# Two early blocks convolved in one burst of 64x32 tiles, with x copied inside SBUF, the channel taps made behind block 0, and half of one unit's stores on GpSimd's queue

## The chip, the cores and the metric

The kernel runs on one core of a Trainium2 chip. The core has a matrix engine (TensorE, PE in the profile; PEld is its weight load, which overlaps the matmuls), a vector engine (VectorE, DVE), a scalar engine (ScalarE, ACT), a general engine (GpSimd, POOL) and a queue engine (SyncE, SP), which issues DMAs here and computes nothing. GpSimd issues DMAs too. All DMAs run on the same 16 DMA engines. The metric is the device time of the whole program in microseconds; a lower time is better.

## The reference

```python
def _attn_ref(x, weight):                      # x (8, 4096, 192), weight (8, 7)
    w = softmax(weight, axis=-1)               # with 1e-9 added to the sum
    x_pad = np.concatenate([zeros((B, 6, D)), x], axis=1)
    idx = np.arange(S)[:, None] + np.arange(K)[None, :]
    x_unf = x_pad[:, idx, :].reshape(B, S, K, H, group)
    return np.einsum('hk,bskhg->bshg', w, x_unf).reshape(B, S, D)

def _moe_ref(x, w_gate, w_val, w_out):         # (32768, 192), (192, 1536) twice, (1536, 192)
    g = x @ w_gate
    return (g * (1.0 / (1.0 + np.exp(-g))) * (x @ w_val)) @ w_out
```

First a causal convolution over 7 tokens: 8 heads of 24 channels, one softmaxed tap vector for each head. Its result goes through a SwiGLU feed-forward layer with 192 channels and 1536 hidden units. The output has 32768 rows of 192 in fp32.

## The kernel before

The 32768 tokens are cut into 64 blocks of 512 tokens, and four blocks make a unit. The hidden units are cut into 12 chunks of 128. A step n is one chunk of one block: block n // 12, chunk n % 12. There are 768 steps.

In each step gate_val (lines 837 to 858) does six matmuls of 64 rows by 512 columns, three into a "gate" bank of PSUM and three into a "val" bank, two at a time in the two row halves of the array. ScalarE takes the Silu of the gate bank (L855), VectorE multiplies it with the val bank (L857). There are three gate and three val banks. The down projection of a block is done in four slots (slot, down, lines 862 to 938), one in every third step, with 24 short matmuls each (L872). So TensorE's steady work is three steps and a slot, over and over.

The input of gate_val is the convolved block with channels on the partitions, in three tiles xc0 to xc2. How it is made depends on the block:

- Blocks 0 and 1 (early, eturn): x is loaded in windows of 64 rows (52 tokens and 6 of overlap) into xe. TensorE convolves it with the matrices "wide" (64 rows, 64 columns; the taps are held as a high and a low fp16 part, index a, so two matmuls add up), ScalarE and VectorE copy the result from PSUM into tme, TensorE transposes it (L490), and the engines copy it into xc.
- Blocks 2 and 3 (early_pair, lines 415 to 456): the same from xp, in two bursts of 32 matmuls with 64x64 tiles (tile_position (64r, 64c), so four at a time). The first burst stands after step 13's gate_val, the second inside the slot of step 15. Each burst writes one gate and one val bank, and these are copied (L445, and L456 for a repeat of the first 64 channels). Block 2 is then turned by TensorE (eturn(2) at step 18). Block 3 goes to DRAM (eout, L463, at step 16) and comes back by DMA transposes (efetch, L473, at step 19).
- Blocks 4 to 7, unit 1 (conv_half, lines 515 to 556): x in windows of 32 rows (26 tokens and 6 of overlap), held twice, in partitions 0 to 31 and again in 32 to 63 (and 64 to 95, 96 to 127 for the second half). The matrix "band" holds the high parts of the taps in the first 32 rows and the low parts in the next 32, so that one matmul of 64 rows does both. Its tiles are 64x32, eight at a time. make_band (L363) copies band from wide on GpSimd. The halves run in the slots of steps 25 and 31; then nine stores write the result to DRAM (conv_out, L567 and L575, at steps 31 and 32), and twelve DMA transposes fetch it (fetch, L589, from step 32).
- Blocks 8 to 63 (units 2 to 15, "pooled"): x is cast to fp16 in DRAM by a GpSimd DMA (cast_x, L649), brought to channel-major tiles by DMA transposes (turn_x, L665), channels 128 to 191 of two blocks are joined in one tile (join_x, L669), and the seven taps are multiplied and added by ScalarE (L742), VectorE (L717) and GpSimd (L692, L707) with a tap for each channel. These channel taps are both_taps. They come from make_picks (L609, at step 34; it uses which and above, made by GpSimd at L210 and L218) and make_channel_taps (L620 and L627, at step 37): a matmul with a 0/1 matrix that gives each channel its head's taps.

Order. Every engine runs its instructions in the order of the program text: seq (line 73) chains each one to the one before it on its engine. DMAs stand in that order on the queue of the engine that issues them: SP has the stores, the transposes and the outputs, GpSimd has the loads that cast. A queue that waits holds all that follows on it. For the pooled units, planned (lines 782 to 809) says at which step a unit's DMAs and jobs are put in: for unit 2 cast 21, jobs 38, and ten times for its turns and joins (24 to 42). pooled_work takes ScalarE's and VectorE's part of the jobs one at a time in the chunks j of 1, 4, 7 and 10.

Loads at the start, on GpSimd's queue in this order: xe(0), weights 0 and 1, xe(1), weights 2, the output weights, then the four helper operations for which and above, xp (two loads), x16 of unit 1 (four loads, since both copies of each half come from DRAM), the four copies of make_band, and xs of unit 2.

Of the kernel before, what the change touches and what calls it, by code (L numbers as in the profile page):

```python
# [10 lines left out]
def kernel(  # L11
# [9 lines left out]
    nc = tc.nc  # L21
    fp32 = mybir.dt.float32
# [121 lines left out]
    def dup_x(u, queue=None):  # L144
        for r in range(2):
            p0 = Q * r
            seq(
                (queue or nc.sync).dma_start(
                    out=x16[u][p0 + 32 : p0 + 64], in_=x16[u][p0 : p0 + 32]
                )  # L150
            )
# [46 lines left out]
    load_w(0)  # L198
    load_w(1)
# [5 lines left out]
    which = {}  # L205
    above = {}
    for name, first, rows in (("c01", 0, P), ("c2", P, Q)):
        which[name] = small(f"which_{name}", [H, P], i32)
        seq(
            nc.gpsimd.iota(  # L210
                which[name],
                pattern=[[0, P // rows], [1, rows]],
                base=first,
                channel_multiplier=-grp,
            )
        )
        above[name] = small(f"above_{name}", [H, P])
        seq(nc.gpsimd.tensor_single_scalar(above[name], which[name], 0, op=ALU.is_ge))  # L218
    xp = cpool.tile([P, 2 * EG, D], fp16, tag="xp", name="xp", bufs=1)
    for r in range(2):  # L220
        windows(xp, Q * r, (2 + r) * TB, EO, 0, 2 * EG)
    x16_tile(1)
    for r in range(2):
        for low in (0, 32):
            load_x(1, r, low=low)
# [189 lines left out]
    def early_pair(hh):  # L415
        w = EG * grp
        if hh == 0:
            for e in (2, 3):
                tme[e] = cpool.tile([P, EG, 4 * Q], fp16, tag="tme", name="tme")
        banks = [  # L420
            ppool.tile([P, TB], fp32, tag=tag, name="cv") for tag in ("gate", "val")
        ]
        for t in range(4):
            h = 4 * hh + t
            for a in range(2):
                for c in range(2):
                    for r in range(2):
                        seq(
                            nc.tensor.matmul(  # L429
                                banks[r][Q * c : Q * c + Q, t * w : t * w + w],  # L430
                                wide[Q * r : Q * r + Q, a, h, :],
                                xp[
                                    Q * r : Q * r + Q,
                                    c : 2 * EG : 2,
                                    h * grp : h * grp + grp,
                                ],
                                start=(a == 0 and t == 0),
                                stop=(a == 1),
                                skip_group_check=True,
                                tile_position=(Q * r, Q * c),  # L440
                            )
                        )
        for r, copy in ((0, act), (1, dve)):
            seq(
                copy(  # L445
                    tme[2 + r][
                        :, :, 4 * grp * hh : 4 * grp * hh + 4 * grp
                    ].rearrange("p g (t e) -> p g t e", t=4),
                    banks[r][:, 0 : 4 * w].rearrange(
                        "p (t g e) -> p g t e", t=4, g=EG  # L450
                    ),
                )
            )
        if hh == 0:
            for e in (2, 3):
                seq(dve(tme[e][:, :, SL * Q : 4 * Q], tme[e][:, :, 0:Q]))  # L456

    def eout(e):
        scre[e] = dpool.tile([XW, 4 * Q], fp16, tag="scre", name="scre")
        rows = scre[e].rearrange("(g c j) d -> c j g d", c=2, j=EO)  # L460
        for c in range(2):
            seq(
                nc.sync.dma_start(  # L463
                    out=rows[c], in_=tme[e][Q * c : Q * c + EO, :, :]
                )
            )
# [12 lines left out]
    def eturn(b, where):  # L479
        tiles = [  # L480
            cpool.tile([P, XW], fp16, tag=f"xc{k}", name=f"xc{k}", bufs=8)
            for k in range(SL)
        ]
        turned = range(SL) if len(where) == SL else (0, 2)
        banks = {}
        for k, (pool, tag) in zip(turned, where):
            bank = banks[k] = pool.tile([P, EG, P], fp16, tag=tag, name="turn")
            for g in range(EG):
                seq(
                    nc.tensor.transpose(  # L490
                        bank[:, g, :], tme[b][:, g, Q * k : Q * k + P], ident
                    )
                )
        whole = ((dve, 0, 0, 0, 0, P), (act, 1, 0, 1, 0, P), (dve, 2, 0, 2, 0, P))
        halves = (
            (dve, 0, 0, 0, 0, P), (act, 2, 0, 2, 0, P),
            (dve, 1, 0, 0, Q, Q), (act, 1, Q, 2, 0, Q),
        )
        for copy, k, p0, src, p1, rows in whole if len(banks) == SL else halves:
            seq(  # L500
                copy(
                    tiles[k][p0 : p0 + rows].rearrange(
                        "p (g c j) -> p g c j", c=2, j=EO
                    ),
                    banks[src][p1 : p1 + rows].rearrange(
                        "p g (c q) -> p g c q", c=2
                    )[:, :, :, 0:EO],
                )
            )
        xc[b] = tiles  # L510

# [49 lines left out]
    def conv_out(u, m):  # L561
        r, c = divmod(m, 4)
        t0 = NG * CO * m
# [3 lines left out]
            nc.sync.dma_start(  # L567
# [37 lines left out]
    def make_picks():  # L605
        for name in which:
            pick[name] = small(f"pick_{name}", [H, P], fp16)
            seq(
                nc.vector.scalar_tensor_tensor(  # L609
                    pick[name], which[name], float(grp), above[name],  # L610
                    op0=ALU.is_lt, op1=ALU.mult,
                )
            )

    def make_channel_taps():
        bank = ppool.tile([P, TB], fp32, tag="gate", name="ctap")
        for m, name in enumerate(pick):
            for a in range(2):
# [6 lines left out]
                )  # L625
        both_taps = small("both_taps", [P, 2 * K])
        seq(nc.scalar.copy(both_taps, bank[:, 0 : 2 * K]))  # L627
# [154 lines left out]
    def planned(v):  # L782
# [4 lines left out]
        if v == 2:  # L787
            head, cast, jobs = 10, 21, 38
# [3 lines left out]
            times = (24, 24, 24, 36, 36, 39, 39, 42, 42, 42)  # L792
# [165 lines left out]
    make_wide()  # L958
    early(0, (gate_bank, gate_bank, val_bank))
    eturn(0, (*acc_banks, gate_bank))  # L960
# [4 lines left out]
    for n in range(n_steps):  # L965
# [3 lines left out]
        if n == 15:  # L969

            def work():
                early_pair(1)
# [8 lines left out]
        if n == 13:  # L981
            early_pair(0)
# [16 lines left out]
        elif n == 16:  # L999
            eout(3)  # L1000
        elif n == 19:
            efetch(3)
        if n == 34:
            make_picks()
        if n == 37:
            make_channel_taps()
# [65 lines left out]
```

## Time and profile before

| | us |
|---|---|
| time, median of 3 runs | 773.52 (773.24 to 773.58) |
| profiled execution, its own time | 772.68 |
| profiled execution, span from first to last instruction | 770.9 |
| busy in the span: PE, PEld | 764.5, 673.9 |
| busy in the span: DVE, ACT, POOL | 697.3, 645.1, 618.1 |

Mean times of one instruction, from the table of groups: a gate or val matmul 376 ns (two run side by side), L857 683 ns, L855 597 ns, L872 243 ns (pipelined), L717 1068 ns, L742 715 ns. DMA queues: SP's (q1) moved 60.24 MB in 127824 packets, GpSimd's (q0) 15.77 MB in 12944. The granted clock of TensorE was 0.999 of full speed over the span.

The page has six parts: busy time of each engine, the span in 40 slices (each digit is a tenth of busy time), the DMA queues, the chain of work that ended last, the costliest groups of instructions, and the DMA issues. A timeline row gives start and duration in us, engine (a q marks its queue), line, operation, names written and read, shapes and count, and in brackets the idle time before it and what ended it. Idle time of an engine that is off the chain costs nothing by itself.

### The profile page before, as it was taken

The page shows a single profiled execution, that of the slowest core. Times are in us where ns is not written, and L with a number is a line of the kernel's source. Part 1 is how long each engine was busy: PE and PEld are TensorE (multiplying, and loading weights), DVE is VectorE, ACT ScalarE, POOL GpSimd, SP SyncE. Part 2 cuts the span into 40 slices and gives each one's busy share as a digit, 9 for nine tenths or more (in the row PEclk, how much of TensorE's full clock was granted, in tenths as well). Part 3 has the DMA queues.
Part 4 walks back from the last instruction along what each step waited for, and adds up shares of the span by engine and source line. Part 5 has one row for each costly group of instructions (what it writes and reads, how often), then busy time and mean ns, then how long its engine had stood idle before and what let it go on. Part 6 is the DMA issues. An engine that isn't in the chain of part 4 may idle for free.

```text
span 770.9 us, 27696 instructions
## 1 busy us (share of the span) xinstructions
PE 764.5 (99%) x11041; PEld 673.9 (87%) x11041; DVE 697.3 (90%) x1042; ACT 645.1 (84%) x1107; POOL 618.1 (80%) x557
## 2 busy tenths in 40 slices
PE   8999999999999999999999999999999999999997
PEld 5766688888888888999999999999999999999997
DVE  7778999999999999999999999999999999999775
ACT  6678888888888888888888888888888888888664
POOL 9105889999989898998989989999899998889300
PEclk9999999999999999999999999999999999999999
DMA  9968746653545444456443444336454443221211
GB/s 138 190 131 136 143 77 154 128 87 90 117 85 125 102 86 106 99 99 116 85 107 93 93 118 108 92 84 116 92 118 100 84 116 90 55 67 40 70 57 43
DMA packets 140898, 77.78 MB, mean 101 GB/s; under 512 B 84632, under 2 KB 137632, under 8 KB 140768
## 3 DMA queue, kind: packets, MB, share of 16 engines
q1 hardware_dynamic: 127824, 60.24, 34.3%
q0 software_dynamic: 12944, 15.77, 13.4%
q8 instruction: 86, 1.41, 0.7%
q14 instruction: 44, 0.36, 0.2%
HBM read 31.54 MB, written 37.58 MB: 90 GB/s over the span
## 4 chain that ended last, share of the span: by engine, by line
PE 97%; SPq 1%; ACT 0%; DMA 0%; issue 0%; DVE 0%; ACTq 0%
PE gate L846 32%; PE val L846 32%; PE acc L872 31%; SPq L589 1%; PE warm L946 0%; PE turn L490 0%; SPq L567 0%; PE acc L893 0%; DMA x<-x 0%; PE cv L531 0%; PE cv L386 0%; PE cv L429 0%; ACT tme L404 0%; DVE h L857 0%; ACT wide L344 0%
## 5 line engine op out<-in xcount | busy, mean ns | idle before, releaser
L857 DVE TENSOR_TENSOR h<-sig,val 128x512 f16<-128x512 f16 x768 | 497.6, 683 | 65.5 <-PE gate L846 48.9
L855 ACT ACTIVATE sig<-gate 128x512 f16<-128x512 f32 x768 | 457.5, 597 | 110.4 <-PE gate L846 71.9
L846 PE MATMUL gate<-pxc,w 64*128 64x512 f16 x2016 | 471.2, 376 | 0.0
L846 PE MATMUL val<-pxc,w 64*128 64x512 f16 x2016 | 471.1, 376 | 0.0
L846 PEld LDWEIGHTS <-w 64*128 64x128 f16 x4608 | 397.4, 110 | 65.2 <-issue 1.1
L872 PE MATMUL acc<-wo,h 64*128 64x192 f16 x6096 | 319.2, 243 | 0.2
L872 PEld LDWEIGHTS <-h 64*128 64x128 f16 x6096 | 301.3, 94 | 19.3 <-ACT sig L855 1.1
L692 POOL TENSOR_TENSOR total<-total,part 128x512 f32<-128x512 f32 x168 | 214.1, 1275 | 70.3 <-DVE total L717 50.5
L717 DVE SCALAR_TENSOR_TENSOR total<-x,both_taps,total 128x512 f32<-128x512 f16 x168 | 179.4, 1068 | 0.0
L707 POOL TENSOR_SCALAR piece<-x,both_taps 128x512 f32<-128x512 f16 x168 | 154.5, 920 | 0.0
L692 POOL TENSOR_TENSOR total<-total,piece 128x512 f32<-128x512 f32 x84 | 119.1, 1417 | 7.0
L742 ACT ACTIVATE part<-x,both_taps 128x512 f32<-128x512 f16 x168 | 120.0, 715 | 0.0
L692 POOL TENSOR_TENSOR pxc<-total,piece 128x512 f16<-128x512 f32 x56 | 71.6, 1279 | 4.7
L846 PE MATMUL val<-xc,w 64*128 64x512 f16 x288 | 68.5, 376 | 0.0
L846 PE MATMUL gate<-xc,w 64*128 64x512 f16 x288 | 68.2, 377 | 0.0
L742 ACT ACTIVATE total<-x,both_taps 128x512 f32<-128x512 f16 x84 | 60.0, 714 | 1.2 <-DMA x<-x 1.2
L692 POOL TENSOR_TENSOR y<-total,piece 128x512 f16<-128x512 f32 x28 | 35.6, 1273 | 2.3
L930 DVE COPY o_sb<-acc 128x384 f32<-128x384 f32 x63 | 34.6, 549 | 0.0
L929 ACT COPY o_sb<-acc 128x384 f32<-128x384 f32 x63 | 29.7, 471 | 3.3 <-PE acc L872 3.3
L559 POOL COPY tm<-tm 128x1280 f16<-128x1280 f16 x1 | 1.3, 1251 | 17.4 <-DVE tm L548 17.4
L649 POOL DMA_DIRECT2D xs<-in_x_dram x14 | 8.5, 606 | 0.0
L946 PE MATMUL warm<-fill 128*128 128x512 f16 (+1 forms) x12 | 4.2, 510 | 1.0 <-DVE fill L92 1.0
(73 smaller groups left out, 65.1 us busy)
## 6 DMA issues: line engine op xcount, KB each, us to landing
out_dram<-o_sb SPq DMA_DIRECT2D x63, 384.0 KB
pxc<-pxc SPq DMA_DIRECT2D x112, 64.0 KB
pxc<-y SPq DMA_DIRECT2D x112, 64.0 KB
xs<-in_x_dram POOLq DMA_DIRECT2D x7, 774.0 KB, 6.8
xs<-in_x_dram POOLq DMA_DIRECT2D x7, 768.0 KB, 6.7
x<-in_x_dram POOLq DMA_DIRECT2D x4, 480.0 KB, 11.0
x<-x SPq DMA_DIRECT2D x28, 66.0 KB
x<-xs SPq DMA_TRANSPOSE x112
```

Of the source, the lines that this page charges most:

```text
L589: nc.sync.dma_start_transpose(out=t[:, 0:TB], in_=scr[u][TB * i : TB * i + TB, Q * k : Q * k + P])
L649: nc.gpsimd.dma_start(out=flat[skip * D : rows * D].rearrange("(a n) -> a n", n=n), in_=bass.AP(tensor=x_flat.tensor, offset=(u * UT - XP ...
L692: nc.gpsimd.tensor_tensor(job["dst"] if k == K - 1 else total, total, part, op=ALU.add)
L707: nc.gpsimd.tensor_scalar(part, shifted(k), scalar1=job["tap"][:, k : k + 1], scalar2=1.0, op0=ALU.mult, op1=ALU.mult,)
L717: nc.vector.scalar_tensor_tensor(job["total"], shifted(k), job["tap"][:, k : k + 1], job["total"], op0=ALU.mult, op1=ALU.add,)
L742: nc.scalar.activation(part, shifted(k), AF.Copy, scale=job["tap"][:, k : k + 1])
L846: nc.tensor.matmul(o, w16[m][p0 : p0 + Q, k, e::E], xc[b][k][p0 : p0 + Q, 0:TB], start=(k == 0), stop=(k == SL - 1),)
L855: silu[n] = seq(nc.scalar.activation(sg, g, AF.Silu)).ins
L857: seq(nc.vector.tensor_tensor(hj, sg, v, op=ALU.mult))
L872: nc.tensor.matmul(acc[b][bank][:, s, :], hj[p0 : p0 + Q, ts(2 * bank + s, P)], wo16[p0 : p0 + Q, j, :], start=(not second and j == 0 and ...
L929: seq(nc.scalar.copy(o_sb[:, 0:2, :], acc[b][0]))
L930: seq(nc.vector.tensor_copy(o_sb[:, 2:4, :], acc[b][1]))
```

## The change

- early_pair is one burst, inside the slot of step 15; the call at step 13 goes. It reads xp in windows of 32 rows (20 windows of 26 tokens in place of 10 of 52) and uses band in place of wide: for each of 8 heads, 4 column groups and 2 row halves one matmul with a 64x32 tile. It takes two gate and two val banks at once and copies them afterwards.
- xp is loaded into partitions 0 to 31 and 64 to 95 by GpSimd's queue, and two SP DMAs copy these rows to 32 to 63 and 96 to 127 (twice). x16 of unit 1 is now loaded once and copied in the same way, by dup_x(1) at step 16.
- eout stores four groups of 26 rows in place of two of 52; eturn's copies for block 2 follow the same cut.
- make_picks compares one iota (head_of, made by GpSimd ahead of the second weight load) with the partition number, on VectorE ahead of block 0's convolution. The matmuls of make_channel_taps run behind block 0's transposes, and both_taps is copied behind block 0's copies. The four GpSimd operations for which and above go, and so do the operations at steps 34 and 37.
- conv_out issues every second of the eight groups from GpSimd's queue (odd m), the others and the remainder from SP.
- Unit 2: jobs 34 in place of 38, and the first join at step 32 in place of 36.

```diff
+    def twice(t):
+        for p0 in (0, Q):
+            seq(nc.sync.dma_start(out=t[p0 + 32 : p0 + 64], in_=t[p0 : p0 + 32]))
+
+    def dup_x(u):
+        twice(x16[u])
...
     load_w(0)
+    head_of = small("head_of", [H, D], i32)
+    seq(nc.gpsimd.iota(head_of, pattern=[[1, H], [0, grp]], base=0, channel_multiplier=0))
     load_w(1)
...
-    xp = cpool.tile([P, 2 * EG, D], fp16, tag="xp", name="xp", bufs=1)
+    xp = cpool.tile([P, 4 * EG, D], fp16, tag="xp", name="xp", bufs=1)
     for r in range(2):
-        windows(xp, Q * r, (2 + r) * TB, EO, 0, 2 * EG)
+        windows(xp, Q * r, (2 + r) * TB, CO, 0, 4 * EG)
+    twice(xp)
     x16_tile(1)
     for r in range(2):
-        for low in (0, 32):
-            load_x(1, r, low=low)
+        load_x(1, r)
...
-    def early_pair(hh):
+    def early_pair():
...
+        for hh in range(2):
+            banks = [
+                ppool.tile([P, TB], fp32, tag=tag, name="cv") for tag in ("gate", "val")
+            ]
+            sets.append(banks)
+            for t in range(4):
+                h = 4 * hh + t
+                for c in range(4):
                     for r in range(2):
                         seq(
                             nc.tensor.matmul(
-                                banks[r][Q * c : Q * c + Q, t * w : t * w + w],
-                                wide[Q * r : Q * r + Q, a, h, :],
+                                banks[r][32 * c : 32 * c + 32, t * w : t * w + w],
+                                band[Q * r : Q * r + Q, h, :],
                                 xp[
                                     Q * r : Q * r + Q,
-                                    c : 2 * EG : 2,
+                                    c : 4 * EG : 4,
                                     h * grp : h * grp + grp,
                                 ],
...
-                                tile_position=(Q * r, Q * c),
+                                tile_position=(Q * r, 32 * c),
...
-        rows = scre[e].rearrange("(g c j) d -> c j g d", c=2, j=EO)
-        for c in range(2):
+        rows = scre[e].rearrange("(g c j) d -> c j g d", c=4, j=CO)
+        for c in range(4):
             seq(
                 nc.sync.dma_start(
-                    out=rows[c], in_=tme[e][Q * c : Q * c + EO, :, :]
+                    out=rows[c], in_=tme[e][32 * c : 32 * c + CO, :, :]
                 )
             )
...
+        queue = nc.gpsimd if m % 2 else nc.sync
...
-            nc.sync.dma_start(
+            queue.dma_start(
...
-            head, cast, jobs = 10, 21, 38
+            head, cast, jobs = 10, 21, 34
...
-            times = (24, 24, 24, 36, 36, 39, 39, 42, 42, 42)
+            times = (24, 24, 24, 32, 36, 39, 39, 42, 42, 42)
...
+    make_picks()
     early(0, (gate_bank, gate_bank, val_bank))
-    eturn(0, (*acc_banks, gate_bank))
+    eturn(0, (*acc_banks, gate_bank), make_channel_taps)
     make_band()
...
         if n == 15:
-
-            def work():
-                early_pair(1)
+            work = early_pair
...
-        if n == 13:
-            early_pair(0)
...
         elif n == 16:
             eout(3)
+            dup_x(1)
         elif n == 19:
             efetch(3)
-        if n == 34:
-            make_picks()
-        if n == 37:
-            make_channel_taps()
```

## The prediction

> **What bounds the kernel now.** I read the page first, then the chain of waits over 44 to 66 us, the weight-load timeline of TensorE over the first 74 us, and the queues of SP and GpSimd over the same stretch. The page:
>
> ```profile
> span 770.9 us, 27696 instructions
> PE   8999999999999999999999999999999999999997
> DMA  9968746653545444456443444336454443221211
> PE 97%; SPq 1%; ACT 0%; DMA 0%; issue 0%; DVE 0%; ACTq 0%
> ```
>
> TensorE is the chain for 97% of the span; the only other part of any size is SP's queue, 1%. The DMA row matters for what follows: the 16 engines are full in the first two slices (to 38 us) and never again.
>
> The timeline of weight loads shows what TensorE pays for the work that the change touches. Columns: start, duration, engine, line, operation.
>
> ```profile
> 20.12 1.18 PEld L872 LDWEIGHTS <-h 64*128 64x128 f16 x23
> 22.19 0.46 PEld L429 LDWEIGHTS <-wide 64*64 64x64 f16 x32 [0.41 <-issue]
> 23.85 0.77 PEld L872 LDWEIGHTS <-h 64*128 64x128 f16 x12
> 24.77 0.46 PEld L429 LDWEIGHTS <-wide 64*64 64x64 f16 x32 [0.16 <-issue]
> ...
> 49.31 1.14 PEld L872 LDWEIGHTS <-h 64*128 64x128 f16 x24
> 50.61 0.16 PEld L620 LDWEIGHTS <-pick_c 8*128 8x128 f16 x4 [0.16 <-issue]
> 52.56 1.14 PEld L872 LDWEIGHTS <-h 64*128 64x128 f16 x24
> ...
> 61.36 1.14 PEld L872 LDWEIGHTS <-h 64*128 64x128 f16 x24
> 64.81 0.94 PEld L872 LDWEIGHTS <-h 64*128 64x128 f16 x24 [0.62 <-ACT sig L855]
> 67.54 1.14 PEld L872 LDWEIGHTS <-h 64*128 64x128 f16 x24
> ```
>
> The L872 groups are a clock: undisturbed they start 2.93 us apart (58.42 to 61.36; 3 steps and one quarter of a down projection). 20.12 to 23.85 is 3.73, so the first burst of early_pair costs 0.80. 49.31 to 52.56 is 3.25, so the channel-tap matmuls cost 0.32. 61.36 to 67.54 is 6.18 where two intervals are 5.87, so a wait costs 0.31. Its cause is on ScalarE and SP:
>
> ```profile
> 46.36 5.81 SPq L567 DMA_DIRECT2D scr<-tm  x8
> 52.21 0.60 SPq L575 DMA_DIRECT2D scr<-tm  x1
> 52.87 8.54 SPq L589 DMA_TRANSPOSE xc<-scr  x6
> 61.45 0.60 SPq L669 DMA_DIRECT2D x<-x  x1
> ...
> 63.55 0.73 ACT L742 ACTIVATE total<-x,both_taps 128x512 f32<-128x512 f16 x1 [1.18 <-DMA x<-x]
> ```
>
> SP issues back to back from 46.36; the join at L669 stands behind nine stores and six transposes, ScalarE waits for it, and the next Silu is late for TensorE.
>
> **The change, part by part.** The sum is made against the profiled execution: span 770.9, 772.68 around it. The median of the runs shown is 773.52, which is 0.84 above; I carry differences over to the median.
>
> *One burst in place of two (PE).* Removed: 0.80 at 22 us and 0.77 at 25 us (the Silu behind it comes 2.41 after the one before, against 1.64 in an undisturbed slot), 1.57 together. Added: one burst of again 64 matmuls of 120 columns. The nearest row is conv_half (L531, in the same timeline at 36.85): the same 64x32 tiles, two bank sets, four copies; from its L872 group at 36.05 to the next at 39.75 is 3.70, so it costs 0.77 with 32 loads in 0.47 us. Ours has twice the loads and half the columns: the 64 loads of block 1 (L386) took 0.63, so 0.77 + 0.16 = 0.93 at most; at least 0.77. I take 0.85. Gain 0.72 (0.64 to 0.80). "Eight at a time" alone buys little: each count stays 64. VectorE gets both copies (0.65 each) and the two 0.25 copies in a row before h of step 16, ending about 1.4 us after the burst; that h waits for its Silu longer than that, so I cost it at nothing; without that cover it is up to 0.3.
>
> *Channel taps behind block 0.* Minus 0.32 at 50 us. The four loads (0.16) now lie after block 0's transposes, where weight loads pause from 8.64 to 8.74 and again, after the first pair, 8.89 to 9.22 for ScalarE's copy of xc1: hidden. The ScalarE copy (0.17) falls into the 0.68 it idles before the first Silu. Two VectorE comparisons stand in the 0.48 that it idles before 7.36; ident (128 columns) took 0.28, pick_c (128 columns) 0.27, so 192 and 64 columns are about 0.35 + 0.2, or 0.08 more than the gap, in a chain that TensorE waits for: plus 0.08 (0 to 0.15).
>
> *GpSimd's queue.* The four helper operations (12.83 to 14.46) go, one iota (about 0.3) comes ahead of the second weight load. Weights and xe(1) move back 0.3 in issue; xe(1) lands about when block 1 starts (13.98), but the DMA engines are full there and landing follows them, not the issue: nothing, at most 0.25. The loads of xp are issued about 1.3 us earlier, x loads are two instead of four, the xs load comes about 3 us earlier.
>
> *Half of the stores by GpSimd.* SP issues five instead of nine before its transposes, about 2.9 us less. GpSimd idles from 40.3 to 60.97, four issues of about 0.8 lie in that; where that cover is gone its adds wait 3 us, which the 20 us forgive. The join also moves ahead of the second fetch (3.8 us). ScalarE asks for it three steps earlier (jobs 34, not 38), about 2.9 us, and SP is about 2.9 + 3.8 us earlier: the wait goes. Minus 0.31 (0 to 0.31). The next late thing would be the x01 turn for block 1, issued after the second fetch, needed nine steps later: not on the path. xs of unit 3 is now issued after the second job, about 4 us later; its transposes feed work at step 91, 100 us: nothing.
>
> *x doubled in SBUF, the new wait.* The burst at step 15 reads rows 32 to 63 and 96 to 127 of xp, which two SP DMAs of 240 KB fill once each load has landed. TensorE wants them at 24.77 - 0.80 + 0.08 = 24.05. All of gate, val and down work stands behind the waiting matmul, so a late copy costs its full lateness. The second xp load was issued at 15.3 and landed at 21.5; earlier issue helps only as far as the full DMA engines let it, so I take 20.9. What an SP DMA then takes is not shown for this size. From below: the join (66 KB) at 61.45 took 2.02 on quiet engines; 174 KB more at about 200 GB/s is 0.9: landed 23.8, no wait. From above: the stores of block 3, two of 130 KB, behind the same kind of x loads:
>
> ```profile
> 26.17 0.78 SPq L463 DMA_DIRECT2D scre<-tme  x2
> 36.85 4.85 SPq L473 DMA_TRANSPOSE xc<-scre  x3
> ```
>
> ```profile
> q0 software_dynamic: 1769, 0.67, 158.6%
> ```
>
> The second fence is the queue table of 26.2 to 29.8 us: GpSimd's queue moved 1769 packets, and SP's queue, with its stores issued, has no row: not one packet in 3.6 us. Their reader went only at 36.85. By this row the copy is 20.9 + 3.6 + 1.2 (240 KB at 200 GB/s) + about 0.4 to the semaphore = 26.1, a wait of 2.05; with the landing no earlier than before, 2.65. The copy's case is nearer to this row, with the x loads queued ahead of it, but there are two of them and not four, so the block can end sooner: I take 1.6 (0 to 2.65).
>
> The Trainium skill (DMA: Bandwidth & Descriptors, Anatomy of one DMA) gives a DMA a fixed 2.0 us plus its bytes at 436 GB/s. By it the copy would need an estimated 2.6 us, no wait would be left, and the change would be a plain gain of 1.27. The scre row, over 10 us for 260 KB, disagrees, since the rule knows no loads ahead.
>
> x16's copies (480 KB each) are issued some 4 us after the burst, behind the stores of block 3, and needed 11.5 us after it (25.3 to 36.85 now). On quiet engines 4 + 1.7 (the join's 2.02 less its 66 KB) + 4.8 (960 KB at 200 GB/s) = 10.5 is in time; by the scre row 4 + 3.6 + 4.8 + 0.4 = 12.8 is 1.3 late. The x loads are over by then, so I take nothing.
>
> Sum: 770.9 - 0.72 - 0.32 - 0.31 + 0.08 + 1.6 = 771.23, that is 0.33 more: 773.85 on the median.
>
> **The rivals.** A: the copies land in time, as after quiet issues. For it: the join's 2.02, the earlier loads. Against it: no SP packet in 3.6 us. Sum -1.27: 772.25; with the burst as cheap as 0.63 (the bare loads of L386) and the comparisons free, 0.30 less: 771.95; with part of the 0.52 that TensorE's loads idle for a Silu at 27.32 gone too, 771.5. B, the slower side: the copies are served only once the x loads have drained (the second x load landed at 26.7 before), so 26.7 + 1.2 + 0.4 = 28.3, a wait of 4.25: 773.52 - 1.27 + 4.25 = 776.5. It decides from a landing after 26.9. For it: SP's stores got their first packet only near the landing of the third x load. Against it: after that they shared the engines with the fourth. C: the wait for the join stays, or x16's copies are late for conv_half at 37 us: 0.3 to 1.3 more than the forecast, 774.15 to 775.15. That the change doesn't do what it says, eight at a time being no faster, is in the 0.85 already.
>
> **How the numbers follow.** 0.2% is 1.55 us, about what a measurement of this kernel can tell from no change. Forecast (wait of 0.6 to 2.65, 772.9 to 774.9): 0.46. A: 0.29, of it 0.15 beyond -1.55. B: 0.20, all beyond +1.55. C: 0.05, of it 0.02 beyond +1.55. So faster 0.15, slower 0.22, same 0.63. The range leaves out the far side of A and most of B: 772.0 to 775.6; the likeliest case's own range is 772.9 to 774.9.
>
> **What would show it.** Right: no L429 group at 22 us, one burst of 64 near 25.6 with TensorE idle before it, released by the DMA of xp; L872 starts 2.93 apart from 47 us on, with no x<-x wait on ScalarE; nothing but transposes at the start for the taps. Wrong: a burst at 24.0 without idle time (then A), a burst after 27 (B), idle time before L531, or any L872 interval after 75 us other than 2.93, for which I have no term.

## The result, and the profile after

| | before | after |
|---|---|---|
| time, median (runs) | 773.55 us (773.17 to 775.37, 6) | 777.4 us (776.9 to 779.9, 6) |
| profiled execution, its own time | 772.68 | 777.33 |
| span of it | 770.9 | 775.6 |

The changed kernel is slower: ratio 1.0054, 95% interval 1.0038 to 1.007. The kernel before took over 775 us (775.07 to 777.73) in 15 of the 87 executions that were timed beside the changed kernel and the runs below; none of these has a trace, so what lengthens them is open. The page of the changed kernel has these lines in answer to those of before:

```profile
span 775.6 us, 27705 instructions
PE   8999999999999999999999999999999999999997
DMA  9964756544354353454434444353554533221211
PE 96%; DMA 3%; POOL 1%; issue 0%; ACT 0%; POOLq 0%
```

TensorE is still nearly all of the chain, but DMA is in it now, with 3%, and SP's queue, 1% before, is not. The chain over 12 to 34 us names the transfers (columns: start, duration, what):

```profile
14.94 6.78 DMA xp<-in_x_dram
...
21.74 6.58 DMA xp<-xp
...
28.45 0.75 PE cv L420 x63
```

The second load of xp is issued at 14.94, when xe(1) has landed (14.66), and lands at 21.73; SP issues the second SBUF copy at once, and it takes 6.58 us until it has landed; then the burst runs. The timeline of TensorE's weight loads shows what that costs (L420 is the new burst, L876 the down projection, which was L872):

```profile
23.76 0.77 PEld L876 LDWEIGHTS <-h 64*128 64x128 f16 x12
27.15 0.09 PEld L420 LDWEIGHTS <-band 64*32 64x32 f16 x1 [2.62 <-issue]
28.42 0.64 PEld L420 LDWEIGHTS <-band 64*32 64x32 f16 x63 [1.18 <-issue]
29.14 0.44 PEld L876 LDWEIGHTS <-h 64*128 64x128 f16 x12
...
51.66 1.14 PEld L876 LDWEIGHTS <-h 64*128 64x128 f16 x24
54.60 1.14 PEld L876 LDWEIGHTS <-h 64*128 64x128 f16 x24
...
63.40 1.14 PEld L876 LDWEIGHTS <-h 64*128 64x128 f16 x24
66.33 1.14 PEld L876 LDWEIGHTS <-h 64*128 64x128 f16 x24
```

One matmul goes at 27.15, when the first copy is in, the other 63 at 28.42, after the second. Behind 50 us all is as forecast: 2.93 us between L876 groups, with neither the 0.32 of the tap matmuls nor the 0.31 of the join in it.

There is a second loss, which only the granted clock shows. The busy time of the engines, us by us (columns: stretch, its length, the busy time of PE, PEld, DVE, ACT and POOL in it with their instruction counts, then the granted clock, the DMA share and GB/s):

```profile
26.00:27.00 1.00, 0.00 (x0) 0.00 (x0) 0.00 (x0) 0.00 (x0) 0.00 (x0) 1.00 1.05 289
30.00:31.00 1.00, 1.00 (x8) 0.43 (x6) 0.53 (x1) 0.00 (x0) 0.00 (x0) 0.50 0.22 49
```

TensorE stands still in the first stretch; in the second it is busy, but at 0.50 of its clock, which it has from 29.75 to 33.16 us.

The Silu of each of the 768 steps is in every trace, so a kernel is compared with the one before step by step: a step's time is the time from its Silu's start to that of the next. The spans' 4.65 us come from:

| where | us | how read |
|---|---|---|
| start to the first Silu | +0.45 | 10.29 against 9.84; TensorE's full clock starts at 5.86 us, not 4.41 |
| step 6 | +0.25 | xe(1)'s second load landed at 14.66, not 13.92 |
| step 13 | -0.79 | the first burst is gone |
| steps 15 to 17, burst | +0.26 | a burst of 1.03 (second run below) for one of 0.77 |
| steps 15 to 17, wait | +3.66 | from L876 (23.76) to the 63 loads 4.66, against 0.92 unhindered in the second run below; the rest of the burst 0.08 shorter than there |
| steps 15 to 17, clock | +1.45 | from 29.14 to the transposes of block 2 at 34.34: 5.20, against 3.75 in that run |
| step 37 | -0.32 | tap matmuls gone |
| steps 49 to 52 | -0.32 | wait for the join gone |

No other step moves by more than 0.03. On the medians the difference is 3.85, since the profiled execution of before is 0.87 under its median and that of after 0.07 under its own.

### The profile page after: what moved, and what is told of

Same layout as the page of the kernel before. It is cut to its first block, busy times and chain, and to the rows that moved or that the text cites. A ratio compares the mean times of both kernels' runs of the same rounds, so it can differ in the third digit from the quotient of the medians.

```text
span 775.6 us, 27705 instructions
## 1 busy us (share of the span) xinstructions
PE 765.9 (99%) x11041; PEld 632.1 (82%) x11041; DVE 697.6 (90%) x1042; ACT 645.1 (83%) x1107; POOL 618.4 (80%) x556
## 4 chain that ended last, share of the span: by engine, by line
PE 96%; DMA 3%; POOL 1%; issue 0%; ACT 0%; POOLq 0%
PE gate L850 48%; PE acc L876 32%; PE val L850 15%; DMA xp<-in_x_dram 1%; DMA xp<-xp 1%; DMA xe<-in_x_dram 1%; POOL w L166 0%; POOL xe L98 0%; PE acc L897 0%; PE cv L528 0%; PE cv L420 0%; PE turn L483 0%; ACT o_sb L1038 0%; POOL jn L190 0%; POOL head_of L199 0%
## 5 line engine op out<-in xcount | busy, mean ns | idle before, releaser
L850 PEld LDWEIGHTS <-w 64*128 64x128 f16 x4608 | 354.8, 110 | 95.8 <-issue 1.6
L876 PEld LDWEIGHTS <-h 64*128 64x128 f16 x6096 | 284.8, 94 | 31.6 <-issue 0.6
L876 PE MATMUL acc<-wo,h 64*128 64x192 f16 x6096 | 306.8, 243 | 0.0
L746 ACT ACTIVATE part<-x,both_taps 128x512 f32<-128x512 f16 x168 | 117.1, 714 | 0.0
L565 POOL DMA_DIRECT2D scr<-tm x4 | 2.6, 647 | 5.3 <-ACT tm L545 5.3
```

The lines of the kernel that those rows point to most:

```text
L565: queue.dma_start(out=scr[u][t0 : t0 + full * CO, :].rearrange("(g j) d -> j g d", j=CO), in_=tm[u][32 * c : 32 * c + CO, NG * r : NG * r ...
L746: nc.scalar.activation(part, shifted(k), AF.Copy, scale=job["tap"][:, k : k + 1])
L850: nc.tensor.matmul(o, w16[m][p0 : p0 + Q, k, e::E], xc[b][k][p0 : p0 + Q, 0:TB], start=(k == 0), stop=(k == SL - 1),)
L876: nc.tensor.matmul(acc[b][bank][:, s, :], hj[p0 : p0 + Q, ts(2 * bank + s, P)], wo16[p0 : p0 + Q, j, :], start=(not second and j == 0 and ...
```

## The experiments

Theory 1: SP's copies of xp are served late because GpSimd's loads of x and xs are queued ahead, TensorE waits for them, and the clock falls because TensorE stands still. Beside the first four runs the kernel before took 773.1.

**The x loads issued after the copies have landed.** Only what is queued ahead is undone:

```diff
...
-    twice(xp)
-    x16_tile(1)
-    for r in range(2):
-        load_x(1, r)
+    copies = twice(xp)
...
     make_band()
+    x16_tile(1)
+    for r in range(2):
+        load_x(1, r, copies[1].ins)
```

> The changed kernel, but unit 1's two x loads are issued by GpSimd only once the second copy of xp has landed (they stand behind the copies of band, and xs stands behind them). Theory 1 (SP's copies of xp wait for the x loads queued ahead of them on the DMA engines): the second copy lands about 2.6 us after its issue in place of 6.6, near 24.3 us; TensorE waits under 0.5 us at the burst, the granted clock stays 1.0, and the time falls by the wait (3.8) and the half clock (1.5) to about 772.3. Theory 2 (copies of 32 rows of 7680 B are slow by themselves): the copy still takes 5 to 6.6 us on quiet engines, the wait stays at 2.5 us or more, the time at 775.5 to 777.4.

Measured: 779.29 us, ratio 1.007 (1.0046 to 1.0094). Its timeline of weight loads (L419 is the burst, L527 conv_half):

```profile
24.02 0.81 PEld L419 LDWEIGHTS <-band 64*32 64x32 f16 x64 [0.16 <-issue]
...
38.12 0.09 PEld L527 LDWEIGHTS <-band 64*32 64x32 f16 x1 [1.83 <-DMA x<-x]
42.51 0.58 PEld L527 LDWEIGHTS <-band 64*32 64x32 f16 x31 [4.31 <-issue]
```

At the burst theory 1 holds: the copies, issued at 19.29 and 21.02, had their packets at 20.57 to 21.88 and 22.20 to 23.58, and all 64 weights load in one go at 24.02. The total fails, because the wait is moved: x16's loads now run from 24.64 to 36.04, with xs of unit 2 behind them. Block 3's stores, issued at 26.32, got their first packet at 30.39, and x16's first copy, which stands behind them on SP's queue, at 34.75. Steps 25 to 28 take 7.63 us more than before.

**xp loaded twice from DRAM, no copy of it.**

```diff
-        windows(xp, Q * r, (2 + r) * TB, CO, 0, 4 * EG)
-    twice(xp)
+        for low in (0, 32):
+            windows(xp, Q * r + low, (2 + r) * TB, CO, 0, 4 * EG)
```

> The changed kernel with both halves of xp's rows loaded from DRAM by GpSimd (four loads of 240 KB in front of the x loads) and no SP copy of xp. Theory 1: two more loads cost 2 x 1.3 us of DMA time, the fourth lands near 24.3 us, the wait at the burst is under 0.5 us and the clock stays full: about 772.3. A third theory (xp itself comes too late, because its second load waits for xe(1)'s landing at 14.66): the burst still waits 2 us or more, 775 or above.

Measured: 772.77 us, ratio 0.9993 (0.9979 to 1.0007). The wait is gone, and with it the whole loss:

```profile
24.42 0.72 PEld L420 LDWEIGHTS <-band 64*32 64x32 f16 x64 [0.16 <-issue]
...
36.77 0.09 PEld L528 LDWEIGHTS <-band 64*32 64x32 f16 x1 [0.16 <-issue]
37.75 0.36 PEld L528 LDWEIGHTS <-band 64*32 64x32 f16 x31 [0.90 <-issue]
```

The first line is the unhindered burst; the Silu behind it comes 2.67 us after the one before, 1.03 more than in a slot without one. The other two show x16's SBUF copies late in their turn: their packets ran from 30.77 to 36.78, and steps 25 to 28 take 0.89 too long.

**The wait kept, TensorE busy in it.** 14 matmuls of zeros by 512 columns into a spare bank ahead of the burst:

```diff
...
-            work = early_pair
+
+            def work():
+                spare = ppool.tile([P, TB], fp32, tag="gate", name="spare")
+                keep_warm(14, into=spare)
+                early_pair()
```

> The changed kernel with 14 matmuls of 512 columns of zeros (3.0 us) in the slot of step 15 ahead of the burst, into a spare gate bank. The wait for the copies stays as it is. If the half clock from 29.75 to 33.16 us comes of the idle 3.8 us, it is gone and the time falls by about 1.5 to 775.9. If it comes of something else (the burst, the tiles), it stays and the time is 777.4 or a little more.

Measured: 775.57 us, ratio 1.0023 (1.0007 to 1.0038), 1.83 below the change, or 1.38 when each is taken against the kernel before beside it. The stretches that were shown of the change above:

```profile
26.00:27.00 1.00, 1.00 (x6) 0.37 (x4) 0.00 (x0) 0.00 (x0) 0.00 (x0) 1.00 1.11 302
30.00:31.00 1.00, 1.00 (x10) 0.34 (x6) 0.44 (x1) 0.59 (x1) 0.00 (x0) 1.00 0.23 45
```

TensorE is busy, the clock stays at 1.00, and the 63 weights load at 28.34, as late as in the change. So the wait costs by itself, and the half clock comes from standing still. In the steps, 15 to 17 are 0.88 shorter than in the change: the 1.45 is gone, but TensorE came to the wait 0.67 earlier here, and the copies no earlier, so the wait is 0.57 longer.

**The taps alone, on the kernel before:** make_picks ahead of block 0, make_channel_taps behind its transposes, head_of for which and above.

```diff
...
+    make_picks()
     early(0, (gate_bank, gate_bank, val_bank))
-    eturn(0, (*acc_banks, gate_bank))
+    eturn(0, (*acc_banks, gate_bank), make_channel_taps)
...
-        if n == 34:
-            make_picks()
-        if n == 37:
-            make_channel_taps()
```

> The kernel before with the channel taps alone moved: head_of on GpSimd, the comparisons and the four matmuls at block 0, no operations at steps 34 and 37. My theory: the interval that holds the tap matmuls goes from 3.25 to 2.93 (minus 0.32), block 0's first Silu comes 0.07 later at an equal clock, and xe(1) lands up to 0.7 later, so that block 1's burst waits 0.1 to 0.3: the sum is between -0.25 and +0.05, 773.3 to 773.6. Rival: the late xe(1) of the changed kernel is not of this part, and block 1 waits for nothing: 773.3.

Measured: 773.23 us, ratio 1.0003 (0.9985 to 1.0021), which tells nothing of a third of a us. The steps do: step 37 is 0.32 shorter, and so are steps 49 to 52, though all nine stores are still SP's: the join was issued at 60.94, 0.51 earlier than before. Block 1 waits for nothing (step 6 is as before; xe(1) landed at 14.13), so the rival is right: the late xe(1) of the change is not of this part. The first Silu came at 10.49; but in the first and third run, with the same taps, at 9.88, and there the full clock had started at 5.12 and 4.72 us, here at 6.38.

The next runs were made to find a version without the loss. Beside them the kernel before took 773.26.

**No SBUF copy at all:** as the second run, and x16 too loaded twice from DRAM.

```diff
     for r in range(2):
-        load_x(1, r)
+        for low in (0, 32):
+            load_x(1, r, low=low)
...
             eout(3)
-            dup_x(1)
```

> The change with no SBUF copy at all before step 16: both halves of xp and both halves of unit 1's x16 loaded from DRAM by GpSimd (4 loads each); the single burst, the early taps and the split stores stay. Theory 1 (what cost the time are copies queued on SP behind GpSimd's loads; with xp loaded twice, the 0.89 us that step 25 still took too long, 3.29 us against 2.40 between two Silus, was the x16 copy): the Silu of step 26 starts 2.40 us after that of step 25, step 15 to 16 stays at 2.67, and against before only gains are left, 1.03 for one burst instead of 0.80 + 0.77 (-0.54), -0.32 for the taps and -0.32 for the join: about 772.4 us (772.1 to 772.9, the upper part if the clock comes up late at the start). Rival (the wait moves once more, to the loads): four xp loads ahead push the x16 loads so far back that the last lands after the first half of unit 1's convolution wants it at 36.8 us; step 25 to 26 stays above 3 us and the time is 773.0 to 773.8.

Measured: 775.21 us, ratio 1.0031 (1.0018 to 1.0044). Steps 25 to 28 are as before, so the 0.89 was the x16 copy; but steps 70 to 75 take 3.91 us more, half clock included, and step 19 takes 0.34 more, for which the trace names no releaser. Neither the theory nor the rival had this.

**Every part but the doubling:** before's xp with 64x64 tiles, in one burst; x16 as before; taps and stores as in the change. The cut is against the change:

```diff
-    xp = cpool.tile([P, 4 * EG, D], fp16, tag="xp", name="xp", bufs=1)
+    xp = cpool.tile([P, 2 * EG, D], fp16, tag="xp", name="xp", bufs=1)
...
-    twice(xp)
...
-                for c in range(4):
-                    for r in range(2):
...
+                for a in range(2):
+                    for c in range(2):
+                        for r in range(2):
...
+                                    wide[Q * r : Q * r + Q, a, h, :],
...
-            dup_x(1)
```

> Every part of the change but the doubling: xp as before (64 x 64 tiles, two halves loaded from DRAM, no copy), x16 loaded twice from DRAM as before, but one burst at step 15, taps behind block 0, and half of the stores by GpSimd. Theory 1: the doubling gave nothing and the other parts give -1.2 us: 772.4 us (772.1 to 772.9), with the burst (64 matmuls, as with the smaller tiles) at 1.0 us, step 15 to 16 at 2.6 to 2.7 us. Rival: the smaller tiles were worth something by themselves, and the burst with 64 x 64 tiles costs 0.80 + 0.77 = 1.57 us as the two did: step 15 to 16 at 3.2 us and 773.0 us.

Measured: 774.95 us (772.21 to 778.19), ratio 1.0026 (1.0011 to 1.0042). Step 15 takes 2.83, above the 2.6 to 2.7 of theory 1 and well under the rival's 3.2: a burst of 64x64 tiles costs 1.19, where one of 64x32 tiles cost 1.03. The time lies 2 us and more above both: in the traced execution (775.0) steps 70 to 74 take 2.22 too long. The 12 executions lie far apart, so this wait need not be the same in each. The timeline of GpSimd, SP and ScalarE there:

```profile
77.32 0.64 POOL L654 DMA_DIRECT2D xs<-in_x_dram  x1
78.12 0.47 SPq L674 DMA_DIRECT2D x<-x  x1
85.96 0.72 ACT L747 ACTIVATE total<-x,both_taps 128x512 f32<-128x512 f16 x1 [3.08 <-DMA x<-x]
```

The join, 66 KB, is issued 0.80 us behind the load of unit 3's x (774 KB) and is there for ScalarE 7.8 us later. In the run before this one the two were issued at 80.02 and 77.50. In the change the order is the other way round, by 0.84 us, and the join costs nothing:

```profile
81.46 0.51 SPq L673 DMA_DIRECT2D x<-x  x1
82.30 0.64 POOL L653 DMA_DIRECT2D xs<-in_x_dram  x1
```

Before, the load was issued at 67.60, 14 us ahead of the join. It is the same mechanism as at the burst, at another place: in the eleven traces in which the load is not running when this join is issued, the join's first packet comes 1.13 to 1.16 us later; in these two it comes 4.23 and 3.41 us later. It is the plan (jobs from step 34) that put the load behind GpSimd's second job, near the join: in the seven traces with this plan the two issues are 0.5 to 2.5 us apart, in five with the join first and in these two with the load first.

**One burst alone, and the stores alone, on the kernel before** (in the first, early_pair is written as in the run above):

```diff
...
-                early_pair(1)
+                early_pair()
...
-        if n == 13:
-            early_pair(0)
```

> Before, with one edit: the two bursts of blocks 2 and 3 (steps 13 and 15) made one at step 15, 64 x 64 tiles and xp as before, no copy. Steps 13 to 14: 0.65 us between two Silus instead of 1.44. If one burst costs what the prediction took (0.85 us), step 15 to 16 takes 2.49 us (2.41 before, and 1.64 without a burst) and the gain is 0.72 us; if it costs what the run with xp loaded twice showed for the smaller tiles (1.03), 2.67 us and 0.54 us. If merging saves nothing, 3.2 us.

```diff
+        queue = nc.gpsimd if m % 2 else nc.sync
...
-            nc.sync.dma_start(
+            queue.dma_start(
```

> Before, with one edit: every second of unit 1's eight stores by GpSimd; the due times of the plan (jobs from 38, join at 36) are left as they were. Theory 1 (the wait at the join, 0.32 us between steps 49 and 53, is the SP queue's: eight stores of 0.4 us each ahead of the join): steps 49 to 53 take 4.57 us instead of 4.89. Rival (it went because the changed plan starts the jobs at 34 and the join at 32, not because of the queue): steps 49 to 53 stay at 4.89 us.

Measured, in one execution each: 776.83 and 772.69 us. With one burst, step 13 is 0.79 shorter and step 15 takes 2.83 (a burst of 1.19), so 0.37 is gained, between merging's forecast of 0.54 and nothing; but the first join, issued at 62.72 instead of 61.45, let ScalarE start only at 66.03, and steps 49 to 52 take 4.04 more, half clock included. With the stores alone steps 49 to 52 are 0.32 shorter, which theory 1 expected. Taps alone did the same. In all thirteen traces this first join had its first packet 1.24 or 1.25 us after its issue; so whether it is late depends above all on when SP comes to issue it.

**The plan of before put back** into the version without the doubling:

```diff
-            head, cast, jobs = 10, 21, 34
+            head, cast, jobs = 10, 21, 38
...
-            times = (24, 24, 24, 32, 36, 39, 39, 42, 42, 42)
+            times = (24, 24, 24, 36, 36, 39, 39, 42, 42, 42)
```

> The run with every part but the doubling (one burst, xp and x16 as before, taps early, stores split), with the plan of before put back: unit 2's jobs from step 38 and its join at 36 instead of 34 and 32. Theory 1 (a transfer of SP that is issued behind a load of GpSimd waits until that load is through: in that run the second join was issued 0.80 us after unit 3's x load, and in the run with no copies 2.5 us after, and steps 70 to 74 took 2.1 and 3.9 us too long, while where the join was first, as in the change, there was no wait): with the old plan unit 3's x load is issued near 68 us as before (67.6), some 10 us ahead of the second join, has landed by then, and no step from 70 on takes longer than before. Left are -0.37 (one burst of 1.20 instead of 0.80 + 0.77), -0.32 and -0.32: 772.5 us (772.1 to 773.0, by when the clock comes up at the start). Rival (the join is late for another reason, the order on GpSimd itself): steps 70 to 74 stay 2 us too long, 774.5 us. Second rival: with jobs from 38 the first join is late again, as before and as in the run with one burst alone: steps 49 to 53 over 4.57 us by 0.3 to 4 us, 772.8 to 776.5.

Measured: 773.04 us, ratio 0.9986 (0.9971 to 1.0002). Unit 3's load is issued at 67.55 and no step from 70 on waits, as theory 1 said; the second rival is true too: the first join is issued at 62.08, and steps 49 to 52 are 0.71 longer.

**Only one of the x loads ahead of the copies:** the change, with the second load held until the second copy has landed.

```diff
-    twice(xp)
+    copies = twice(xp)
...
-    for r in range(2):
-        load_x(1, r)
+    load_x(1, 0)
...
     make_band()
+    load_x(1, 1, copies[1].ins)
```

> The change, with the second of unit 1's two x loads held until xp's second SBUF copy has landed (and unit 2's x load behind it); the first x load is queued ahead of the copies as in the change. Theory 1 (the copies get no packet before the load that is queued ahead of them is through; in the change the first copy packet went out at 24.64 us, 0.36 after the first x load landed): the first copy packet still goes out within 0.5 us after the first x load has landed, at 24 to 25 us, but the copies then have the queues to themselves and last 1.3 to 2.7 us as in the run with both loads behind the copies; the burst waits about 2 us instead of 4.2 and the clock keeps its full speed: about 775 us. Rival 1 (the copies share the queues from their issue on and are slowed by whatever is in flight): the first packet goes out within 2.2 us of the issue at 20.5, and the burst waits under 1 us: 773 to 774. Rival 2 (the delay has nothing to do with the x loads): first packet at 24.6, last at 27.7 and burst at 28.4 as in the change: 777.

Measured: 781.09 us (one execution), 7.19 of it at x16's copies in steps 25 to 28, as in the first run. The first copy packet went out at 22.90, 1.30 after the issue at 21.60 and 2.1 before the x load landed (25.04). So the expectation is wrong as it was written, and rival 1's sign came, though the burst waited 2.4 us and not under 1. The packets tell why. The DMA table of 22.6 to 24.5 us (columns: queue, packets, MB, time of the packets as a share of the 16 engines):

```profile
q1 hardware_dynamic: 70, 0.42, 94.0%
q0 software_dynamic: 60, 0.02, 10.0%
```

In the 1.8 us to 22.4 GpSimd's queue (q0) had moved 806 packets; here it moves 60, so of the load only stragglers were left, and SP's queue (q1) had the engines. A load's landing can come well after the bulk of its packets. The table of the change for 20.6 to 24.5 us, by contrast, has only this row:

```profile
q0 software_dynamic: 1931, 0.76, 163.0%
```

**The join at 32, the jobs at 38,** in the version with the plan of before:

```diff
-            times = (24, 24, 24, 36, 36, 39, 39, 42, 42, 42)
+            times = (24, 24, 24, 32, 36, 39, 39, 42, 42, 42)
```

> As the run with the old plan (every part but the doubling; unit 2's jobs from step 38), with one number changed: the first join at step 32 instead of 36, as in the change. In the run before this one the first join was issued at 62.08 us, behind three transposes of SP more than in the change, and steps 49 to 53 took 5.6 us. Theory 1 (both joins are on SP in order, and each costs nothing if it is ahead of what is queued there and no load of GpSimd is in flight): the first join is issued near 58 us, steps 49 to 53 take 4.57 us, unit 3's x load stays near 68 us, ahead of the second join by 10 us, and no step from 70 on waits: against before -0.40 (burst), -0.32 and -0.32, 772.2 us (771.7 to 772.9, by the clock's start), that is at or just below the kernel before, the fastest of these kernels. Rival (the first join's wait goes to the transposes that it is moved ahead of): another step between 49 and 60 takes over 0.3 us more than before, and the time stays at 773.0.

Measured: 772.5 us (771.97 to 773.92, 12 runs), against 773.19 for the kernel before beside it: ratio 0.9984, 95% interval 0.9971 to 0.9997. The first join is issued at 57.64, unit 3's load at 67.53, the second join at 81.85, and no step waits: -0.79 + 0.43 (burst) -0.32 -0.32, that is -1.00. The traced execution shows none of it in its span (771.0), since its first Silu is 0.63 late and the end behind the last Silu takes 0.50 longer. It is the fastest of these kernels and beats the one before by 0.16% in the ratio and by 0.69 us, 0.09%, in the medians.

## Why the prediction was wrong

**The failed step is "x doubled in SBUF, the new wait".** It took 1.6 us between 0 and 2.65; the wait was 3.66. Its upper bound was made of a landing at 20.9, 3.6 without a packet, 1.2 of copying and 0.4 to the semaphore, 26.1 together. Measured, in the same order: 21.73; 2.91 until the first packet at 24.64; 3.03 until the last at 27.67; 0.75 until the 63 weights at 28.42. TensorE came to the wait at 24.68 (23.76 + 0.92), not 24.05, which takes 0.63 off the wait again.

The silent time was right in size. The copying was not. It was priced as one copy of 240 KB; but the first copy, issued at 20.53, had been held as well, so both had to go when the silence ended. In the first run, with the engines all but free, the two took 1.31 and 1.38, each near the 1.2 of the step, 2.69 together; that leaves 0.34 for sharing the engines with the xs load of unit 2, which the change issues 2 us earlier (19.00 for 21.07). The landing was late because the second xp load, taken to be issued 1.3 us earlier, waited for xe(1) and came only 0.34 earlier. And with a row in hand that showed 3.6 us of silence, the step took a value well inside its bounds because two loads instead of four were queued.

Rival B had the landing, 28.3, and got a chance of 0.20. That its 776.5 is near the measured 777.4 is in part luck: its wait was 4.25, not 3.66, and it had no half clock. Its terms were not quite the chip's either: the copies did not wait for the second x load to land (28.65), but began at 24.64. The Trainium skill's rule of a fixed 2.0 us plus bytes at 436 GB/s (DMA: Bandwidth & Descriptors, Anatomy of one DMA), which spoke for rival A, is fitted there to GpSimd's DMAs. The estimate of 2.6 us that it gives comes near in the first run, where SP's copies of 240 KB landed 2.94 and 3.07 us after their issue, and fails with loads ahead: the second copy of the change took 6.58.

**A term was missing:** 1.45 us at half clock behind the wait. The prediction had every wait cost its lateness and nothing more. With the 2.06 of the wait, 0.45 at the start and 0.25 at step 6 it makes up nearly all of the 4.32 by which the span missed the sum (775.55 for 771.23).

**One burst** was to gain 0.72 (0.64 to 0.80) and gained 0.53: 0.79 went, but the merged burst cost 1.03, above its bound of 0.93. Against one burst of 64x64 tiles (1.14 to 1.20 in four traces) eight at a time is worth 0.11 to 0.17, as little as was said.

**Taps** -0.32: right. The 0.08 for VectorE's comparisons did not show: 9.88 us to the first Silu in the first and third run, with them, and 9.88 with the stores alone, without them.

**xe(1)**, "nothing, at most 0.25": 0.25 at step 6 in the profiled execution of the change, under 0.03 there in all eleven experiments.

**The join** -0.31: right in size. Moving half of the stores is enough for it, but not needed: the taps alone did it as well.

**x16's copies at nothing** came true only by luck: the burst's own lateness let the xs load land (32.30) before they were issued (32.73). In the three runs in which the burst was less late and the copies were made, they cost 0.89 to 7.63. **"xs of unit 3 ... nothing"** was true for its transposes, but the load itself, 14.7 us later and not 4, stood near the join, which the step did not look at.

## What to carry to other kernels

Check in time every small transfer on SP's queue that the critical engine waits for against every long load of GpSimd, also those pairs that a change of plan brings together somewhere else: here, issued while such a load ran, a transfer got its first packet 3.4 to 4.2 us later, against 1.1 to 1.3 without one. If a row shows several us without a packet, price the wait by that row, count every transfer that was held in that time, and see what else is then in flight. A wait of TensorE can cost half clock on top (1.45 us here, for a wait of 3.66), so price both.

## What the runs showed of the hardware

The time from an SP transfer's issue to its first packet (packets told apart by their size) falls into two groups, for transfers with nothing unserved ahead of them on SP's queue:

| kernel, transfer | issued, first packet | us | GpSimd's loads then |
|---|---|---|---|
| change, xp copy | 20.53, 24.64 | 4.11 | running |
| busy wait, xp copy | 19.72, 23.86 | 4.13 | running |
| before, store of block 3 | 26.17, 29.84 | 3.67 | running |
| x loads behind, store of block 3 | 26.32, 30.39 | 4.07 | running |
| one load behind, store of block 3 | 28.59, 32.44 | 3.85 | running |
| all but the doubling, join | 78.12, 82.35 | 4.23 | running |
| no copies, join | 80.02, 83.43 | 3.41 | running |
| one load behind, xp copy | 21.60, 22.90 | 1.30 | packets all but over at 22.4 |
| x loads behind, xp copy | 19.29, 20.57 | 1.28 | all but over |
| change, join | 81.46, 82.62 | 1.16 | none yet |
| fastest version, join | 81.85, 82.98 | 1.13 | none |

The store of block 3 took 3.37 to 4.14 us in all eleven traces in which GpSimd's loads were in full flow, and 0.81 in the other two, the change and the busy wait, where the last load was nearly through when the store was issued.

It is not a wait for the loads to end: the late join got its packets from 82.35 to 83.67 while the x load's ran to 84.08. Whether some 4 us of packets are already lined up ahead, or the issue itself is slowed, stays open. That join was also complete for its reader only at 85.96, 2.3 us after its last packet.

The granted clock changes in stretches of 3.41 us: 29.75 to 33.16 in the change, 39.26 to 46.09 (twice that) in the first run. Counted from the start of the full clock, every change falls on a multiple of 3.413 us, and the busy time of TensorE in these windows tells which of them brought the clock down. Over the thirteen traces it was those in which TensorE was busy for 44% or less by the profile, and none of those with 49% or more. Ahead of a fall it was busy for 44% in the change (1.51 of the 3.42 us from 26.33 to 29.75), 28% in the first run, 33% with one burst alone, 40% with no copies, 8% with one load behind, and 0 to 36% at the end of each program. So the place of a gap counts too: 2.52 us without weight loads before a late Silu halved the clock in the run with no copies, where it lay in one window (40% busy), and did not in the one with all but the doubling, where it was cut by the end of one (91 and 49%). The clock came back behind windows that were 85% busy or more, and not behind one of 75%.

The Trainium skill (TensorE: Matmul & The Clock Gate, Part 1: The HAM clock gate) gives free-running windows of about 3.4 us, after an idle one of which the clock is halved. The lengths here agree, and so does the run kept busy; but the five windows that brought the clock down ahead of the end were not idle: TensorE was busy for 8 to 44% of them.

The start varies in the same way: the full clock came at 4.41 to 6.98 us in the thirteen profiled executions, and the first Silu at 9.84 to 10.51, with every clock start before 5.2 giving 9.84 to 9.88.
